# Stage A of a spectral mixing kernel: casts ahead of copies, other engines for the copies, fewer warming matmuls, one placement moved

## The chip, the cores and the metric

The kernel runs on one core of a Trainium2 chip. The time is the device time of that core in microseconds (us). Before the change it was 764.62 us, the median of three runs (763.43, 764.62, 766.18). The profiled execution has a span of 763.7 us from its first to its last instruction. Engines are called by their names: TensorE (PE in the profile, PEld for its weight loads), VectorE (DVE), ScalarE (ACT), GpSimd (POOL), and SyncE (SP), which issues transfers.

## The reference

Two layers follow each other. The first mixes along the sequence with a filter in the frequency domain, the second is a feed-forward layer with a squared ReLU. In short:

```
X = np.fft.rfft(x, axis=1)                         # x: 8 x 3008 x 256, float32
Y = X * (filt_r + 1j * filt_i)[None]               # filt_r, filt_i: 1505 x 256
y = np.fft.irfft(Y, n=3008, axis=1)
h = np.maximum(y.reshape(24064, 256) @ w_in, 0.0)  # w_in: 256 x 2048
out = h * h @ w_out                                # w_out: 2048 x 256
```

## The kernel before

**The whole.** The sequence length is 3008 = 64 x 47, so the transform is done in two stages with matrices of sines and cosines: stage A transforms along 47, stage B along 64, then comes the product with the filter (`prods`, line 423), and two inverse stages (`unit_p0` or `unit_p`, line 446 or 460, and `unit_y`, line 496). The result `yt` goes into the feed-forward part, 47 groups of 512 tokens. All tiles between are float16. For seven of the eight batches the transform is woven into the feed-forward steps by a plan (`fft_plan`) that gives each unit a due step. Batch 0 has nothing to hide behind: its transform, and the setup of all constants, is the prologue, which takes the first 58 us of the profiled execution and is written out by hand at the end of the kernel. The change lies in this prologue alone.

**Queues.** [...] The order of the calls in lines 738 to 808 is therefore also the order of each engine's queue[...].

**Stage A of batch 0.** x of batch 0 is loaded as float32 into three tiles `xw` (0, 1, 2), each in two halves of 512 KB, in the order of `HALVES`: (0,0), (1,0), (0,1), (1,1), (2,0), (2,1). SyncE issues these six transfers first, then the filter's real and imaginary parts (1504 KB each), small constants, the constants of stage B (`sSB`, `sSP`), and `w_in`. `cast_wide` (line 226) turns a half into float16 on VectorE. Eight units, `unit_a0(c, k)` with c from 0 to 3 and k of 0 or 1, do the transform: each has 16 matmuls of 96 columns (lines 373 and 375) into two banks of PSUM. Units with c of 0 or 2 read `xw16` of tile 0, those with c of 1 or 3 tile 2; all read tile 1 too. The two banks are copied into the tile `uT`: where they are one `psH` tile, both by ScalarE (line 382) or both by VectorE (line 384), in turn; where they are a pair of `psF` or `psO`, the first by ScalarE and the second by VectorE.

**After stage A.** `turn_u(k, eng)`, six times, transposes `uT` by matmuls with the identity (line 392, `psT`) and copies it into `ut` (lines 398 and 400). The filter is cast to float16 in pieces (line 222): the real part by GpSimd and VectorE, the imaginary part by VectorE, GpSimd and ScalarE. `place_f(im, k, ...)` puts a sixth of the real (im 0) or imaginary part (im 1) where stage B's output wants it: matmuls with a selection matrix (line 286, `psf`), then an evacuation into `sF` by ScalarE (line 294) or VectorE (line 298). A placement of the imaginary part needs all three pieces of that part's cast.

**The rounds.** The loop over k from 0 to 6 at line 785 holds two `unit_b` (two matmuls, line 415, and one product on VectorE, line 423), the next imaginary placement, from the second round on a `unit_p0` with its evacuation `ze` on ScalarE (line 448), and in the first three rounds a real placement. `unit_p0` also reads `sSPx`, constants with swapped halves that GpSimd copies (lines 778 and 779), between loads of batch 1. After the rounds `read_z`, four `unit_a` of batch 1, 13 filling matmuls and four `unit_y` lead into the feed-forward loop (line 526).

**Banks of PSUM.** `bank_pair` (line 169) deals out pairs of banks in rotation: two tiles of `psH` (each one tile of two banks, so one evacuation), then a pair of `psF`, then a pair of `psO` (two tiles, so two evacuations). Every `unit_a0`, every `turn_u` and the placements ahead of the rounds take the next pair. Counting from 0, the eight units take 0 to 7, the six turns 8 to 13, the placements ahead of the rounds 14 to 17. Placements inside the rounds and `unit_p0` take `psH`; `unit_b` of batch 0 takes `psF` or `psO`.

**Warming.** While x is on its way, TensorE runs `WARM` matmuls of 512 columns on zeros (line 265).

The functions and the calls follow, with the line numbers of the profile.

Of the kernel before, what the change touches and what calls it, by code (L numbers as in the profile page):

```python
# [20 lines left out]
SLOTS = 8  # L21
CLS = 376
QF = 3008
WARM = 16


def _build_consts():
# [83 lines left out]
def kernel(  # L111
# [9 lines left out]
    nc = tc.nc  # L121
# [38 lines left out]
    def psO(name):  # L160
        return pps.tile([128, 2, 256], F32, tag="psO", name=name, bufs=2)

    def psH(name):
        return pps.tile([128, 2, 512], F32, tag="psH", name=name, bufs=2)
# [4 lines left out]
    def bank_pair(name):  # L169

        k = npair[0] % 4
        npair[0] += 1
        if k < 2:
            t = psH(name)
            return [t[:, 0, :], t[:, 1, :]], [(t, 0)]
        ts = [psF(f"{name}_{i}") if k == 2 else psO(f"{name}_{i}").rearrange("p a d -> p (a d)")
              for i in range(2)]
        return ts, [(t.unsqueeze(1), i) for i, t in enumerate(ts)]

    def pair_engine():  # L180
        return nc.vector if npair[0] % 2 == 0 else nc.scalar
# [39 lines left out]
    def cast(eng, out, in_):  # L221
        (eng.copy if eng is nc.scalar else eng.tensor_copy)(out=out, in_=in_)

    def cast_wide(k, i):
        m = slice(4 * i, 4 * i + 4)
        nc.vector.tensor_copy(out=xw16[k][:, m, :], in_=xw32[k][:, m, :])

    HALVES = ((0, 0), (1, 0), (0, 1), (1, 1), (2, 0), (2, 1))
# [34 lines left out]
    ps = psO("warm").rearrange("p a d -> p (a d)")  # L263
    for _ in range(WARM):
        nc.tensor.matmul(ps, zero, sF[:, 0, 0:2, :], start=True, stop=True)  # L265
# [3 lines left out]
    def place_f(im, k, *engs, rotate=False):  # L269

        if rotate:
            banks, groups = bank_pair(f"psf_{im}_{k}")
        else:
            t = psH(f"psf_{im}_{k}")
            banks, groups = [t[:, 0, :], t[:, 1, :]], [(t, 0)]
        for i in range(4):
            c = 4 * k + i
            e0, e1 = D * c, D * (47 - c)
            cuts = [0] + [d for d in range(1, D)
                          if (e0 + d) % QF == 0 or (c and (e1 + d) % QF == 0)] + [D]  # L280
            for d0, d1 in zip(cuts, cuts[1:]):
                o = banks[i // 2][:, (i % 2) * D + d0:(i % 2) * D + d1]
                low = divmod(e0 + d0, QF)
                up = divmod(e1 + d0, QF) if c else (0, QF + d0)
                for r, (q, a) in enumerate((low, up, low, up)):
                    nc.tensor.matmul(o[32 * r:32 * r + 32, :], sPF[:, q, :],  # L286
                                     f16s[0][:, im, a:a + d1 - d0], start=True, stop=True)
        for t, i in groups:
            n = t.shape[1]
            eng = engs[i % len(engs)]  # L290
            dst = sF[:, im, 4 * k + 2 * i:4 * k + 2 * i + 2 * n, :]
            src = t.rearrange("p t (a d) -> p (t a) d", d=D)
            if eng is nc.scalar:
                eng.activation(out=dst, in_=src, func=AF.Copy, scale=sign[:, 0:1] if im else 1.0)
            elif im:
                eng.tensor_scalar_mul(out=dst, in0=src, scalar1=sign[:, 0:1])
            else:
                eng.tensor_copy(out=dst, in_=src)
# [4 lines left out]
    def load_win():  # L303

        for k, c, n, pool, tag in ((0, 0, 768, p_ze, "ze"), (0, 768, 768, p_ze, "ze"),
                                   (0, 1536, 512, p_prod, "prod"), (1, 0, 768, p_ze, "ze"),
                                   (1, 768, 512, p_prod, "prod"), (1, 1280, 512, p_prod, "prod"),
                                   (1, 1792, 256, p_prod, "prod")):
            t = pool.tile([128, n], F32, tag=tag, name=f"win32_{k}_{c}")
            nc.sync.dma_start(out=t, in_=moe_w_in[128 * k:128 * k + 128, c:c + n])  # L310
            wins.append((t, k, slice(c, c + n)))
# [50 lines left out]
        if b == 1:  # L362
            write_u(b, c)

    def unit_a0(c, k):

        banks, groups = bank_pair(f"psA_0_{c}_{k}")
        for dt in range(2):
            for i in range(4):
                m = 4 * k + i  # L370
                o = banks[dt][:, 96 * i:96 * i + 96]
                d = slice(128 * dt, 128 * dt + 128)
                nc.tensor.matmul(o, xw16[2 * (c % 2)][:, m, d], s0[:, c // 2, :],  # L373
                                 start=True, stop=False)
                nc.tensor.matmul(o, xw16[1][0:120, m, d], s0[0:120, 2 + c, :],
                                 start=False, stop=True)
        for dt in range(2):
            m = 32 * c + 16 * k
            o = uT[:, dt, :, m:m + 16].rearrange("p c (m q) -> p m c q", q=4)
            pv = banks[dt][:, 0:384].rearrange("p (m c q) -> p m c q", m=4, q=4)  # L380
            if (pair_engine() is nc.scalar) if len(groups) == 1 else (dt == 0):
                nc.scalar.copy(out=o, in_=pv)
            else:
                nc.vector.tensor_copy(out=o, in_=pv)

    def turn_u(k, eng):

# [21 lines left out]
    def unit_b(b, p):  # L409
        if b == 0 and p % 4 > 1:  # L410
            ps = psO(f"psB_{b}_{p}").rearrange("p a d -> p (a d)")
        else:
            ps = psF(f"psB_{b}_{p}")
        for i in range(2):
            nc.tensor.matmul(ps[:, i * D:(i + 1) * D], sSB[:, 2 * p + i, :],  # L415
                             uts[b][:, 2 * p + i, :], start=True, stop=True)
        if b == 0:
            if p == 0:
                prods["ring"] = p_y.tile([128, 5, 2, 2, D], F16, tag="yt", name="prods_0")
            prod = prods["ring"][:, p % 5]  # L420
        else:
            prod = p_prod.tile([128, 2, 2, D], F16, tag="prod", name=f"prod_{b}_{p}")
        nc.vector.tensor_mul(  # L423
            out=prod,
            in0=ps.rearrange("p (a d) -> p a d", d=D).unsqueeze(1).to_broadcast([128, 2, 2, D]),
            in1=sF[:, :, 2 * p:2 * p + 2, :])
        prods[(b, p)] = prod
        if b > 0:
            for i in range(2):
                nc.gpsimd.dma_start(out=prod[64 * i:64 * i + 64, 0],  # L430
                                    in_=prod[64 - 64 * i:128 - 64 * i, 1],
                                    accum_op=mybir.AluOpType.add)
# [3 lines left out]
    def unit_p0(k):  # L436

        if k == 0:
            zes[0] = p_h2.tile([128, NC, D], F16, tag="h2", name="ze_0")
        ze = zes[0][:, 4 * k:4 * k + 4, :]  # L440
        ps = psH(f"psP_0_{k}")
        for i in range(4):
            c2 = 4 * k + i
            prod = prods[(0, c2 // 2)]
            for v, w in enumerate((sSP[:, c2, :], sSPx[c2 // 12][:, c2 % 12, :])):
                nc.tensor.matmul(ps[:, i // 2, (i % 2) * D:(i % 2) * D + D], w,  # L446
                                 prod[:, v, i % 2, :], start=(v == 0), stop=(v == 1))
        nc.scalar.copy(out=ze, in_=ps.rearrange("p t (a d) -> p (t a) d", d=D))
        nc.sync.dma_start(
            out=dZ[0].rearrange("(s p) d -> p s d", p=128)[:, 4 * k:4 * k + 4, :],  # L450
            in_=ze)
# [286 lines left out]
    for k in range(2):  # L738
        c = slice(12 * k, 12 * k + 12)
        load_const(sSB[:, c, :], dSB, k)  # L740
        load_const(sSP[:, c, :], dSP, k)
    load_win()
    for k, i in HALVES[:2]:
        cast_wide(k, i)
    unit_a0(0, 0)
    unit_a0(2, 0)
    for k, i in HALVES[2:4]:
        cast_wide(k, i)
    unit_a0(0, 1)
    unit_a0(2, 1)  # L750
    for i in range(2):
        cast_wide(2, i)
        unit_a0(1, i)
        unit_a0(3, i)
    f16s.append(p_h2.tile([128, 2, QF + D], F16, tag="h2", name="f16"))
    for im in range(2):
        nc.gpsimd.tensor_copy(out=f16s[0][:, im, QF:], in_=nyq[:, im, :])
# [8 lines left out]
    turn_u(5, nc.vector)  # L766
    place_f(0, 0, nc.scalar, rotate=True)
    place_f(0, 1, nc.vector, rotate=True)
    place_f(0, 2, nc.scalar, rotate=True)
    for eng, e in ((nc.vector, slice(0, 1024)), (nc.gpsimd, slice(1024, 2048)),  # L770
                   (nc.scalar, slice(2048, QF))):
        cast(eng, f16s[0][:, 1, e], f32s[1][:, e])
# [1 line left out]
    for k in range(6):  # L774
        if k % 3 == 0:
            sSPx.append(p_u.tile([128, 12, 128], F16, tag="u", name=f"sSPx_{k}"))
        c, o = slice(4 * k, 4 * k + 4), slice(4 * k % 12, 4 * k % 12 + 4)
# [7 lines left out]
    for k in range(7):  # L785
        if k < 6:
            unit_b(0, 2 * k)
            if k < 5:
                place_f(1, k + 1, nc.scalar)
            unit_b(0, 2 * k + 1)  # L790
        if k > 0:
            unit_p0(k - 1)
        if k < 3:
            place_f(0, k + 3, nc.scalar)
    read_z(0, 0)
    read_z(0, 1)
    tiny = const.tile([1, 1], F16, name="tiny")
# [16 lines left out]
    for s in range((NG + 1) * SLOTS):  # L814
        g, k = divmod(s, SLOTS)
# [16 lines left out]
        while stores and stores[0][0] <= s:  # L832
            _, i, n, ost = stores.pop(0)
# [31 lines left out]
```

## Time and profile before

| What | Value |
|---|---|
| median time of three runs | 764.62 us |
| span of the profiled execution | 763.7 us |
| TensorE busy, whole span | 742.6 us (97%) |
| TensorE busy, first 60 us | 46.61 us |
| VectorE busy, first 60 us | 36.56 us |
| ScalarE busy, first 60 us | 31.97 us |
| GpSimd busy, first 60 us | 23.40 us |
| mean granted TensorE clock, first 60 us | 0.89 |
| first matmul of stage A | 9.02 us |
| first turn (psT) | 22.89 us |
| first product of batch 0 (prods) | 33.77 us |
| last ze evacuation of batch 0 starts | 49.56 us |
| first feed-forward matmul (psH) | 58.17 us |

The busy shares of a page are means over the whole span, and the prologue is under a tenth of it. It is therefore read from the timeline of each engine: every line has a start, a length, the engine, the source line, output and inputs, the number of merged instructions, and in brackets the idle time ahead of it with what ended it. The view of waits sums such idle times by the pair of who waited and for what. The chain of work that ended last goes back from the last instruction, at each step to what released it; in order of time its lines have a start, a length and what ran. SPq is the queue of SyncE, in which an issue can wait for a transfer that was issued earlier.

### The profile page before, as it was taken

How to read it: one execution, taken by the hardware profiler on the slowest of the kernel's cores; microseconds unless marked ns; L12 is line 12 of the kernel's file. 1: busy time of each engine (PE TensorE's matmuls, PEld its weight loads, DVE VectorE, ACT ScalarE, POOL GpSimd, SP SyncE). 2: the span in 40 equal slices, each digit the busy share in tenths (PEclk: the TensorE clock that was granted, in tenths of full speed). 3: DMA queues.
4: the chain of work that ended last, by engine and by line, in shares of the span. 5: the costliest groups of instructions: out<-in, count | busy, mean ns of one | idle time of the engine just before them, and what ended most of it. 6: DMA issues, size and time to landing. Idle time of an engine off the chain costs nothing.

```text
span 763.7 us, 20209 instructions
## 1 busy us (share of the span) xinstructions
PE 742.6 (97%) x8517; PEld 539.8 (71%) x8517; DVE 656.9 (86%) x732; ACT 563.9 (74%) x803; POOL 191.4 (25%) x265
## 2 busy tenths in 40 slices
PE   6789899999999999999999999999999999999998
PEld 4555666767777776877778777787767777777776
DVE  4677997899989998998989999899989989888773
ACT  2677678777877777787777877777777777777673
POOL 0920561043303232223212324043311222000000
PEclk9799999999999999999999999999999999999999
DMA  9968599657676556854577555865447334321011
GB/s 351 267 160 226 86 188 218 185 108 153 133 220 126 102 112 157 219 124 96 126 179 176 116 124 106 216 140 111 101 116 204 88 73 98 97 74 53 30 56 57
DMA packets 103459, 106.36 MB, mean 139 GB/s; under 512 B 10320, under 2 KB 93520, under 8 KB 102216
## 3 DMA queue, kind: packets, MB, share of 16 engines
q1 hardware_dynamic: 83928, 81.83, 35.4%
q0 software_dynamic: 19296, 23.05, 21.8%
q8 instruction: 67, 1.10, 0.6%
q10 hardware_dynamic: 144, 0.18, 0.1%
q14 instruction: 24, 0.20, 0.1%
HBM read 57.80 MB, written 48.23 MB: 139 GB/s over the span
## 4 chain that ended last, share of the span: by engine, by line
PE 90%; DVE 5%; DMA 2%; ACT 1%; issue 1%; SPq 0%; ACTq 0%; DVEq 0%
PE psH L526 40%; PE psX L641 21%; PE psY L641 16%; PE psB L415 3%; PE psY L496 3%; PE psP L460 2%; PE psA L347 2%; DVE prod L423 1%; PE psO L546 1%; PE warm L265 1%; DVE h L537 1%; DMA dU<-u 1%; PE psf L286 1%; PE psP L446 1%; PE psA L373 1%
## 5 line engine op out<-in xcount | busy, mean ns | idle before, releaser
L530 ACT ACTIVATE h<-psH 128x1024 f16<-128x1024 f32 x376 | 384.9, 1025 | 160.4 <-PE psH L526 158.9
L526 PE MATMUL psH<-yt,sWin 128*128 128x512 f16 (+7 forms) x1728 | 386.8, 351 | 1.2 <-ACT h L530 0.4
L537 DVE TENSOR_TENSOR h<-h 128x2048 f16<-128x2048 f16 (+1 forms) x192 | 229.7, 1197 | 45.7 <-ACT h L530 45.5
L430 POOL DMA_DIRECT2D prod<-prod x168 | 138.7, 968 | 428.3 <-DVE prod L423 425.9
L526 PEld LDWEIGHTS <-sWin 128*128 128x128 f16 x1728 | 149.1, 98 | 90.5 <-issue 3.0
L641 PEld LDWEIGHTS <-sum 128*128 128x128 f16 x2944 | 181.3, 98 | 26.1 <-issue 6.3
L641 PEld LDWEIGHTS <-h 128*128 128x128 f16 x2208 | 135.6, 98 | 24.5 <-issue 5.3
L423 DVE TENSOR_TENSOR prod<-psB,sF 128x1024 f16<-128x1024 f32 x84 | 102.2, 1218 | 11.9 <-PE psB L415 11.8
L641 PE MATMUL psX<-sT,sum 128*128 128x128 f16 x1472 | 104.7, 219 | 0.0
L641 PE MATMUL psY<-sT,sum 128*128 128x128 f16 x736 | 71.2, 219 | 0.0
L641 PE MATMUL psY<-sWout,sum 128*128 128x128 f16 x736 | 56.0, 219 | 1.4 <-DVE bot L656 1.4
L615 DVE TENSOR_TENSOR sum<-sum,h 128x2048 f16<-128x2048 f16 x46 | 56.1, 1220 | 0.8
L195 POOL DMA_DIRECT2D x<-in_x_dram x64 | 56.3, 1053 | 0.5 <-PE psA L347 0.5
L641 PE MATMUL psY<-sWout,h 128*128 128x128 f16 x736 | 56.2, 219 | 0.0
L641 PE MATMUL psX<-sT,h 128*128 128x128 f16 x736 | 56.1, 219 | 0.0
L618 DVE TENSOR_TENSOR sum<-h 128x2048 f16<-128x2048 f16 x46 | 55.9, 1216 | 0.0
L621 DVE TENSOR_TENSOR sum<-h,sum 128x2048 f16<-128x2048 f16 x46 | 55.9, 1215 | 0.0
L612 DVE TENSOR_TENSOR sum<-h 128x2048 f16<-128x2048 f16 x46 | 55.9, 1215 | 0.0
L462 ACT CAST ze<-psP 128x512 f16<-128x512 f32 x84 | 49.2, 586 | 1.2 <-PE psP L460 1.0
L641 PE MATMUL psX<-sWout,h 128*128 128x128 f16 x736 | 48.7, 219 | 0.0
L505 DVE CAST yt<-psY 128x376 f16<-128x376 f32 x62 | 33.6, 542 | 14.0 <-PE psY L496 13.8
L496 PE MATMUL psY<-sC,zt 112*128 112x94 f16 x512 | 42.3, 204 | 0.9 <-DMA zt<-dZ 0.5
(75 smaller groups left out, 558.1 us busy)
## 6 DMA issues: line engine op xcount, KB each, us to landing
zt<-dZ SPq DMA_DIRECT2D x64, 192.0 KB
dU<-u SPq DMA_DIRECT2D x56, 192.0 KB
prod<-prod POOLq DMA_DIRECT2D x168, 64.0 KB, 2.9
dZ<-ze SPq DMA_DIRECT2D x28, 384.0 KB
x<-in_x_dram POOLq DMA_DIRECT2D x48, 192.0 KB, 5.1
ut<-dU SPq DMA_DIRECT2D x7, 1024.0 KB
out_dram<-bot SPq DMA_DIRECT2D x32, 128.0 KB
out_dram<-top SPq DMA_DIRECT2D x16, 256.0 KB
```

What stands on the lines that cost most here:

```text
L195: nc.gpsimd.dma_start(out=t[64 * h + p0:64 * h + p1], in_=v[p0:p1, 8 * c:8 * c + 8, :])
L423: nc.vector.tensor_mul(out=prod, in0=ps.rearrange("p (a d) -> p a d", d=D).unsqueeze(1).to_broadcast([128, 2, 2, D]), in1=sF[:, :, 2 * p:2 ...
L430: nc.gpsimd.dma_start(out=prod[64 * i:64 * i + 64, 0], in_=prod[64 - 64 * i:128 - 64 * i, 1], accum_op=mybir.AluOpType.add)
L496: nc.tensor.matmul(ps[:, 94 * jj:94 * jj + 94], zt[:, 4 * (g % 2) + jj, dt * 128:(dt + 1) * 128], sSY, start=True, stop=True)
L526: nc.tensor.matmul(ps[:, i, o:o + n], sWin[:, dt, jt * 128:(jt + 1) * 128], yts[b][:, dt, r:r + n], start=(dt == 0), stop=(dt == 1))
L530: nc.scalar.activation(out=h2[:, 2 * s:2 * s + 2, :], in_=ps, func=AF.Relu)
L537: nc.vector.tensor_mul(out=v, in0=v, in1=v)
L612: nc.vector.tensor_add(out=t, in0=a21, in1=a22)
L615: nc.vector.tensor_sub(out=t, in0=f[5], in1=a11)
L618: nc.vector.tensor_sub(out=t, in0=a11, in1=a21)
L621: nc.vector.tensor_sub(out=t, in0=a12, in1=f[6])
L641: nc.tensor.matmul(o[:, t, :], f[p][:, q, 128 * t:128 * t + 128], sg["w"][p][:, q, :], start=(m == 0 and p in (1, 2)), stop=(q == 7), skip ...
```

## The change

Four edits, all ahead of the rounds:

1. All six casts of x stand ahead of any copy in VectorE's queue, so that each can run when its half has arrived.
2. `unit_a0` is told which engine copies each bank. The first four units (c of 0 and 2) are copied by ScalarE alone; the last four by VectorE (first bank) and ScalarE (second bank). The matmuls' order stays.
3. Ten warming matmuls instead of sixteen, so that TensorE is free earlier.
4. The fourth real placement, `place_f(0, 3)`, moves from the first round to ahead of the rounds; the real placements in the rounds come in rounds 0 and 1 instead of 0 to 2. As it takes bank pair 17, the first imaginary placement takes pair 18, which is a pair of `psF`, and its evacuation falls into two, one on ScalarE and one on VectorE.

```diff
-WARM = 16
+WARM = 10
...
-    def unit_a0(c, k):
+    def unit_a0(c, k, *engs):
...
-            if (pair_engine() is nc.scalar) if len(groups) == 1 else (dt == 0):
-                nc.scalar.copy(out=o, in_=pv)
-            else:
-                nc.vector.tensor_copy(out=o, in_=pv)
+            cast(engs[dt], o, pv)
...
-    for k, i in HALVES[:2]:
+    for k, i in HALVES:
         cast_wide(k, i)
-    unit_a0(0, 0)
-    unit_a0(2, 0)
-    for k, i in HALVES[2:4]:
-        cast_wide(k, i)
-    unit_a0(0, 1)
-    unit_a0(2, 1)
-    for i in range(2):
-        cast_wide(2, i)
-        unit_a0(1, i)
-        unit_a0(3, i)
+    for c, i in ((0, 0), (2, 0), (0, 1), (2, 1)):
+        unit_a0(c, i, nc.scalar, nc.scalar)
+    for c, i in ((1, 0), (3, 0), (1, 1), (3, 1)):
+        unit_a0(c, i, nc.vector, nc.scalar)
...
     place_f(0, 1, nc.vector, rotate=True)
-    place_f(0, 2, nc.scalar, rotate=True)
+    for k in (2, 3):
+        place_f(0, k, nc.scalar, rotate=True)
...
-        if k < 3:
-            place_f(0, k + 3, nc.scalar)
+        if k < 2:
+            place_f(0, k + 4, nc.scalar)
```

## The prediction

> **What bounds the kernel now.** I read the busy shares first, then the chain that ended last, then the order of time on VectorE, SyncE's queue and TensorE inside the first 36 us, where all edits lie.
>
> ```profile
> PE 742.6 (97%) x8517; PEld 539.8 (71%) x8517; DVE 656.9 (86%) x732; ACT 563.9 (74%) x803; POOL 191.4 (25%) x265
> PE 90%; DVE 5%; DMA 2%; ACT 1%; issue 1%; SPq 0%; ACTq 0%; DVEq 0%
> ```
>
> From about 58 us on, TensorE is the chain almost without a break, and nothing there is edited. So the question is how much earlier the feed-forward part can begin: a time saved ahead of it is passed on whole unless something ahead of it doesn't move along. The chain in order of time shows what sets the pace ahead of it (start, length, what):
>
> ```profile
> 10.66 1.02 DVE uT L384 x2
> 11.68 1.21 DVE xw L226 x2
> 12.94 0.22 PE psA L375
> ...
> 14.54 0.56 DVE uT L384
> 15.10 0.61 DVE xw L226
> 15.76 0.26 PE psA L373
> ...
> 18.54 1.02 DVE uT L384 x2
> 19.56 0.61 DVE xw L226
> ...
> 31.24 0.61 DVE f L222
> 31.90 0.62 PE psf L286 x16
> ```
>
> It is a ladder: VectorE copies one group's results, only then casts the next half of x, TensorE computes on it, VectorE copies. Did the halves arrive that late? SyncE's queue tells: its issues of line 736 each wait for one more half of x (four waits, in the view of waits), so their starts date the landings.
>
> ```profile
> 8.34 0.33 SPq L736 DMA_DIRECT2D sSB<-cSB  x1
> 9.46 0.32 SPq L736 DMA_DIRECT2D sSP<-cSP  x1
> 10.72 0.32 SPq L736 DMA_DIRECT2D sSB<-cSB  x1
> 12.00 0.32 SPq L736 DMA_DIRECT2D sSP<-cSP  x1
> ```
>
> The third to sixth half are there at 8.3, 9.4, 10.7 and 12.0 us. Their casts start at 11.6, about 12.2, 15.02 and 19.48: the last waits 7.5 us behind copies in VectorE's queue. The same reading of line 310's waits gives the filter: real part at 15.6, imaginary part at 19.4 us. In one-microsecond stretches the granted clock is 1.00 up to 15, 0.50 from 16 to 25, and 1.00 again at 26; line 373 follows line 375 at 45 ns in the first and at 80 ns in the second.
>
> [...] 0.50 follows 12 to 15.3, in which TensorE worked some 1.8 us, and ends after 22 to 25.5, in which it worked nearly all the time. The warming matmuls start 0.43 us apart, and the last weight loads come closer together from about 8.6 us, some 6 us after the first: there the clock rose. [...] the trace: 1024 columns from SBUF in 0.69 us, 384 from PSUM in 0.56.
>
> **The change, part by part.**
>
> *Casts ahead.* Six casts of 0.69, each now at its landing (a landing was followed by its cast within 0.1 us for the first two): they end at 5.8, 7.2, 9.0, 10.15, 11.4 and 12.7. Nothing is added; VectorE was idle for 3.44 us ahead of its first copy.
>
> *Warming.* Ten instead of sixteen at 0.43: the end moves from about 9.0 to 6.95, so the first unit can start at 7.26, when the second half is cast. The clock is then still half. [...]
>
> *Stage A.* A unit is 16 matmuls: 0.72 us at 45 ns, 1.28 at 80. Units (0,0) and (2,0): 7.26 to 8.5 and 9.3. Then a wait for the fourth half's cast: units (0,1), (2,1) 10.2 to 11.7. Then (1,0), (3,0) after 11.45: 11.7 to 13.15. Then (1,1), (3,1): 13.15 to 14.6. ScalarE has now 12 copies, in pairs of 0.86 (0.43 each), 0.48 alone: first unit 8.75 to 9.65, second to 10.5, third 11.2 to 12.05, fourth to 12.9, then four single ones, the last at 14.85 to 15.3. That is 5.4 us of copies in 6.6 us, with slack. VectorE's four, 0.47 to 0.56 each, follow its last cast and end with unit (3,1)'s, at 14.8 + 0.56 = 15.35. [...] **Turns start at 15.35** instead of 23.6 (the second psT; the first came at 22.89).
>
> *Turns to the filter casts.* At full clock two turns are 16 matmuls by 56 ns, so VectorE's first turn copy starts 1.1 us later, at 16.5, where it took 25.43 - 23.61 = 1.8 at half clock. From there VectorE ran without a gap from 25.43 to 31.84 (1.14 + 1.07 + 2.33 + 1.20 + 0.67 by the starts): that is 6.4, so 22.9. Its filter cast at 17.6 finds the real part (15.6); GpSimd's half, released by the last cast of x at 12.7 instead of 20.2, is done by 15.6 + 1.44 = 17.1. The imaginary part is there at 19.4, so GpSimd's third is done at 20.5. The filter hides behind VectorE, by 2 to 3 us: no new bound.
>
> *The placement moved ahead.* It costs 0.62 us of TensorE, between others, and one ScalarE evacuation of 1.02. ScalarE's order is: third placement, fourth placement, its piece of the imaginary cast. Before, that piece ended at 31.76, with VectorE's (31.84), so ScalarE had no slack and the new evacuation goes on the path: third placement 20.95 to 21.95, fourth (its bank is free when VectorE's last turn copy ends at 21.1, matmuls to 21.75 or 22.1) to 23.1, cast to **24.1**, against 22.9 without it: 1.2.
>
> *Side effect: banks.* Pairs rotate by four, so the extra placement shifts the first imaginary one from the two-bank tile to the psF pair. Its evacuation splits: ScalarE 0.6, VectorE 0.67 (row of L298) in parallel, instead of 1.11 on ScalarE. But unit_b's first product uses psF too, so its matmuls (0.54), which ran during the evacuation, now follow it. Together 0.1 worse, and the second imaginary placement, queued behind those matmuls on TensorE, comes some 0.7 later against the first product. First product: 24.15 + 0.65 to 0.95 (matmuls) + 0.7 + 0.55 = 26.1 to 26.5, so **26.3** instead of 33.77: 7.5 earlier.
>
> *Rounds.* VectorE's 12 products need 12 x 1.215 = 14.6 us; they took 15.1 (33.77 to 48.89), with 0.38 and 0.68 of gaps where ScalarE's evacuations held a psH bank. One 1.02 fewer in the rounds, less the 0.7 above, leaves the gaps about as they are: 15.0 to 15.2. I book nothing. GpSimd's swapped constants, which end block by block from 24.66 to 35.92, don't move along with the rest, since its transfers and the constants' landings keep their times; but the block for round i is needed only at 29.3, 32.4, 35.4, 37.6, 38.9, 41.4 (lines 446 shifted by 7.5), so each is there. Its weight casts end at 41.2 and are needed at about 50.7.
>
> *Sum:* 7.5 earlier, less 0.1 for small things: 764.6 - 7.4 = **757.2**.
>
> **Rivals.**
>
> *The clock stays half in stage A*[...]. Units take 1.28: 7.26 to 9.8, 10.2 to 12.8, on to 17.9, the turns at 18.7 and VectorE's first turn copy 1.8 later at 20.5: 4.9 ahead of 25.43, less 1.3 for the placement and the banks: 3.6, so 761.0. [...]
>
> *The gain is lost on the way*, in stage B's writes and reads through DRAM, or the feed-forward part starts early and then waits for batch 1's transfers (the chain has 5.69 and 3.84 us of them at 62 to 72). Then nothing or little is left: 764. Against: these transfers are issued behind the evacuations and move with them, and the transfer engines are nearly idle at 36 to 38, so no backlog reaches them.
>
> *Slower: ScalarE's longer list serialises stage A*, each unit waiting for the copies of the one before: 8 x (1.28 + 0.9) = 17.4 from 7.3, so turns at 24.7, 1.1 later than now, plus 1.3 for placement and banks: 767. Against: four pairs of banks rotate, so a unit waits for the copies of the fourth before it.
>
> *Better:* the placement hides after all, and the rounds close their gaps: 1.2 + 0.9 more, 755.1.
>
> **Chances.** Forecast (756 to 758.5) 0.60, half clock in part or whole (758.5 to 761) 0.20, better 0.11, lost 0.05, slower 0.04. For 8 in 10 I take the forecast's case and most of those beside it: 755.2 to 760.3. Faster by over 0.3% (2.3 us) is the first three and a sliver of the fourth: 0.92; within 0.3%: 0.04; slower 0.04.
>
> **What would show it.** Casts of L226 end by 12.8; psA's last matmul at about 14.6 and the first psT near 15.4; clock 1.00 from 8.6 to about 19; four sF evacuations of the real part by ScalarE and VectorE ahead of its imaginary cast, and this cast the last of three; first prods at 26.3; last ze, at 49.56 before, at about 42; first psH, at 58.17, at about 51. If psT starts at 17 to 19 with matmuls of stage A 80 ns apart, the warming was too short. If psT is early but prods aren't, I mis-read the middle part. If psH is early and the end isn't, the loss lies in the feed-forward part, and the prediction is wrong there.

## The result and the profile after

The changed kernel takes **759.95 us** (median of four runs, 759.59 to 761.15). The kernel before, measured beside it, has 764.59 us. The ratio is 0.9941, with a 95% interval of 0.9919 to 0.9962: faster by 4.6 us or 0.6%. The prediction was 757.2 in a range of 755.2 to 760.3. So the direction and the range were right, and 2.8 us of the expected 7.4 did not arrive. Where they went is the subject of what follows.

The profiled executions differ by 6.1 us (spans of 763.7 and 757.6). That of before lies 0.9 above its median and that of after 0.4 below its own, so the two traces show some 1.3 us more than the medians.

The busy shares of the changed kernel's page are within one per cent of those before, and so are the shares of the chain; transfers and ScalarE have one more per cent each:

```profile
PE 89%; DVE 5%; DMA 3%; ACT 2%; issue 1%; POOL 0%; SPq 0%; DVEq 0%; ACTq 0%
```

The ladder is gone. This is VectorE's timeline in the changed kernel (start, length, engine, line, operation, tiles, count, and the idle time ahead with what ended it):

```profile
8.27 0.69 DVE L226 CAST xw<-xw 128x1024 f16<-128x1024 f32 x1 [1.05 <-DMA xw<-in_x_dram]
9.50 0.69 DVE L226 CAST xw<-xw 128x1024 f16<-128x1024 f32 x1 [0.54 <-DMA xw<-in_x_dram]
...
12.04 0.69 DVE L226 CAST xw<-xw 128x1024 f16<-128x1024 f32 x1 [0.58 <-DMA xw<-in_x_dram]
12.65 2.28 DVE L222 CAST uT<-psA 128x384 f16<-128x384 f32 x4
...
25.05 13.81 DVE L420 TENSOR_TENSOR prods<-psB,sF 128x1024 f16<-128x1024 f32 x12 [0.35 <-PE psB L412]
```

Each cast now waits for its half of x and for nothing else, and the twelve products run without a gap. The first turn's matmul starts at 14.98 us instead of 22.89, the first product at 25.05 instead of 33.77. The last evacuation of the rounds (`ze`, which is then written to DRAM as `dZ` and read back as `zt`) starts at 39.54 instead of 49.56. **At the end of the rounds the change is 10.0 us ahead**, more than forecast. Then the lead melts. These are pieces of the chain in order of time, first of the kernel before, then of the changed one (start, length, what):

```profile
49.56 1.02 ACT ze L448
...
50.60 2.42 DMA dZ<-ze
...
53.16 3.43 DMA zt<-dZ
...
56.72 0.33 PE psY L496 x4
```

```profile
39.54 1.02 ACT ze L445
40.58 5.50 DMA dZ<-ze
46.23 3.13 DMA zt<-dZ
...
49.49 0.33 PE psY L493 x4
```

The write of the last `ze` into DRAM takes 5.50 us instead of 2.42; the read behind it takes no longer than before. The first psY with data (the matmuls of `unit_y`, which read `zt`) is 7.2 us ahead, no longer 10.0. In the view of waits, TensorE's wait for this read has grown from

```profile
PE psY L496 <- DMA zt<-dZ: 0.5, 1, 0.5
```

to

```profile
PE psY L493 <- DMA zt<-dZ: 3.3, 1, 3.3
```

A second, smaller loss comes behind it. TensorE has nothing to do in those 3.3 us, and soon after the granted clock is halved for some 3 us. The stretches of the changed kernel, with busy time and instructions of each engine, then the clock, the transfer engines' share and GB/s:

```profile
46.30:49.50 3.20, 0.01 (x1) 0.04 (x2) 0.00 (x0) 0.00 (x0) 1.07 (x2) 1.00 0.78 149
49.50:54.00 4.50, 4.30 (x30) 2.17 (x31) 1.10 (x2) 1.97 (x3) 0.00 (x0) 0.62 1.13 189
```

The first h (ScalarE's evacuation of psH) starts at 52.85 instead of 59.37, 6.5 ahead. The half clock is not over by then. TensorE's timeline shows the first 20 matmuls of psH, in the changed kernel and in a later kernel (e1 below) in which TensorE hardly waits and the clock stays at 1.00:

```profile
50.94 4.18 PE L523 MATMUL psH<-yt,sWin 128*128 128x512 f16 x12 [0.20 <-ACT yt L500]
55.37 1.94 PE L523 MATMUL psH<-yt,sWin 128*128 128x512 f16 x8 [0.25 <-ACT h L527]
```

```profile
48.96 2.04 PE L523 MATMUL psH<-yt,sWin 128*128 128x512 f16 x8 [0.28 <-ACT yt L500]
51.24 1.94 PE L523 MATMUL psH<-yt,sWin 128*128 128x512 f16 x8 [0.25 <-ACT h L527]
53.38 1.02 PE L523 MATMUL psH<-yt,sWin 128*128 128x512 f16 x4 [0.20 <-ACT h L527]
```

From the first psY to the 21st matmul of psH it is 8.0 us in the changed kernel, and 6.9 both before and in e1. So this stretch takes 1.1 us of the lead and leaves 6.1, which is also the lead of the last h (745.8 instead of 751.9).

### The profile page after: what moved, and what is told of

The parts are those of the page before. It is cut to its first block, busy times and chain, and to the rows that moved or that the text cites. A ratio compares the mean times of both kernels' runs of the same rounds, so it can differ in the third digit from the quotient of the medians.

```text
span 757.6 us, 20196 instructions
## 1 busy us (share of the span) xinstructions
PE 737.0 (97%) x8511; PEld 536.0 (71%) x8511; DVE 655.4 (87%) x729; ACT 564.6 (75%) x807; POOL 191.0 (25%) x265
## 4 chain that ended last, share of the span: by engine, by line
PE 89%; DVE 5%; DMA 3%; ACT 2%; issue 1%; POOL 0%; SPq 0%; DVEq 0%; ACTq 0%
PE psH L523 40%; PE psX L638 21%; PE psY L638 16%; PE psB L412 3%; PE psY L493 3%; PE psP L457 2%; PE psA L347 2%; DVE prod L420 1%; DMA xw<-in_x_dram 1%; PE psO L543 1%; DVE h L534 1%; ACT h L527 1%; DMA dZ<-ze 1%; PE psf L286 1%; PE psP L443 1%
## 5 line engine op out<-in xcount | busy, mean ns | idle before, releaser
L534 DVE TENSOR_TENSOR h<-h 128x2048 f16<-128x2048 f16 (+1 forms) x192 | 229.7, 1197 | 46.6 <-ACT h L527 46.1
```

The costliest lines, as they stand in the source:

```text
L534: nc.vector.tensor_mul(out=v, in0=v, in1=v)
```

## The experiments

Each kernel was timed beside the kernel before on the same chip, and the ratios are to that. A profile shows one execution, and it can lie off the kernel's median: 1.8 us above it in e5, 1.9 in e4, 3.2 in e2. Traces of the same code also differ: up to the first product e8 is the kernel before, and this product came at 32.77 us in its trace and at 33.77 in the other. So a difference of about 1 us between two traces says little unless it repeats.

The theory at the start: the lead is lost on the transfer engines, because the load of the first half of `w_out` (`load_wout(0)`, issued by GpSimd in the rounds) kept its time while the rounds moved up to it. The rival: the six writes of the rounds, packed closer together, hold up each other.

### The weight load moved behind the rounds (e1)

```diff
-    load_wout(0)
     cast_win()
...
+    load_wout(0)
     load_wout(1)
```

> The changed kernel with the first weight load (sWout, first half) issued next to the second, after batch 0's first read_z, instead of during the rounds. Theory A (the 10 us won by the end of the rounds shrink to 7 because that load stands on the transfer engines together with the last dZ writes): the last dZ write lands in 2.5 to 3.5 us instead of 5.5, the first real psY starts near 47.5 instead of 49.5, and the time is 1.5 to 2.5 us under the changed kernel's 759.95, so about 758. Theory B (the six dZ writes, packed into 11 us, hold up each other): the last dZ write still takes 5 us, psY stays at 49.5, the time at 760.

Measured: 757.04 us, ratio 0.9901 (0.9886 to 0.9917). The chain in order of time of this kernel:

```profile
40.66 1.02 ACT ze L445
...
41.70 2.38 DMA dZ<-ze
...
44.22 3.15 DMA zt<-dZ
...
47.51 0.33 PE psY L493 x4
```

The last write is back at 2.38 us, although the six writes are as close together as before, and psY starts at 47.5. This kernel even ended its rounds 1.1 us later than the changed one, and still had psY 2.0 earlier. What stood in the way can be seen in the transfers between 38 and 42 us. The columns are packets, MB, and the share of the 16 engines' time. Queue q0 is GpSimd's, q1 SyncE's. First the changed kernel, then e1:

```profile
q0 software_dynamic: 885, 0.45, 93.7%
q1 hardware_dynamic: 694, 0.35, 31.1%
```

```profile
q1 hardware_dynamic: 1263, 0.63, 51.6%
...
q0 software_dynamic: 1, 0.00, 0.0%
```

In the changed kernel the weight load occupies the engines in the stretch in which the last writes of the rounds want them, and it landed at 44.8 us. In e1 it is gone from there. The rival falls. Over the last write's own 5.5 us (40.6 to 46.1), though, the packets of the load's queue took only 20.7% of the engines' time and those of SyncE's queue 59.7%. That points to a backlog: SyncE moved 0.35 MB from 38 to 42 us, against 0.63 in e1, and in those 5.5 us it moved 0.98 MB, of which the last write is 0.26. How the delay divides between the load itself and this backlog is not shown; that it goes when the load goes is.

The moved load returns the second loss as well. In e1 TensorE waits 0.2 us for the read instead of 3.3, the clock stays at 1.00, and the 2.0 us at psY have become 3.1 at the 21st matmul of psH.

### The control: the same move in the kernel before (e8)

> The kernel before with nothing but the moved weight load: the control. Theory A (in the kernel before the load had landed long ahead of the last dZ write, which took 2.4 us): nothing to gain, 764.5 within 0.7, first psY at 56.7. Theory B (the moved load helps the feed-forward part or any prologue): 762 or less, and then the moved load says nothing on where this change's 2.8 us went.

Measured: 764.96 us, ratio 1.0001 (0.9990 to 1.0011). Moving the load gains nothing by itself: the last write took 2.43 us with it and 2.42 without it. Before the change, the load had the same stretch, 38 to 42 us, nearly to itself:

```profile
q0 software_dynamic: 1005, 0.51, 100.5%
q1 hardware_dynamic: 480, 0.24, 20.4%
```

The last write came at 50.6 then, long after it. The first psY of e8 is 1.2 us earlier than before, but 1.0 of that is there at the first product, ahead of the load. So the load's place became a cost only through this change. This cost is shown: e1 is 2.9 us under the changed kernel by the medians and 3.1 by the ratios, and the two intervals do not meet. It is as large as the missing 2.8 us, although it is not the only difference from the forecast (see below).

### The casts alone (e5) and with the moved load (e7)

```diff
-    for k, i in HALVES[:2]:
+    for k, i in HALVES:
         cast_wide(k, i)
     unit_a0(0, 0)
...
-    for k, i in HALVES[2:4]:
-        cast_wide(k, i)
...
-        cast_wide(2, i)
         unit_a0(1, i)
```

> The kernel before with one edit: all six casts of x ahead of the copies (engines of the copies, 16 warming matmuls and placements as before). Theory A (the order in VectorE's queue is the whole ladder): units follow the landings, psT near 16 instead of 22.9, first product near 26.5, and the end of the rounds at about 43; less 1.5 to 3 lost behind the rounds: 760.5. Theory B (the copies by VectorE behind the last cast at 12.7 are a ladder of their own, so the new engines are needed): the copies of the first four units, which wait for the casts, hold their banks, psT comes at 18 or later, and the time is 762 or above.

Measured: 759.71 us, ratio 0.9943 (0.9929 to 0.9957), the same as the whole change. psT started at 16.15, the first product at 25.97, the last `ze` at 41.76. VectorE's copies do pile up behind the last cast, but they don't delay much, as its timeline shows:

```profile
12.80 3.80 DVE L384 CAST uT<-psA 128x384 f16<-128x384 f32 x8
17.70 1.22 DVE L400 CAST ut<-psT 128x1024 f16<-128x1024 f32 x1 [1.10 <-PE psT L392]
```

Eight copies take 3.80 us against four in 2.28 with the new engines: 1.5 us, of which 1.2 is seen at psT. Theory A holds. In its profile this kernel ends its rounds 2.2 us later than the changed kernel, and its last write took less (4.57 us), so that psY comes only 1.3 later. That profile also took 1.9 us longer than the changed kernel's, while the medians are equal, so it does not show why they are. But the load could hide what the other three edits are worth, and e7 takes it away:

> The kernel before with the casts ahead alone (as in the earlier run of that edit) and the first weight load moved behind the rounds. Theory A (the other three edits do bring the rounds to their end some 2 us earlier, and only the transfers behind hid it): the rounds end at 41.8 to 43, first psY at 48.7 to 50, time 758.5 to 759.3, which is 1.5 to 2.3 us above the full change with the moved load (757.0). Theory B (the other three edits are worth nothing): 757.0, the same as with all four.

Measured: 757.97 us, ratio 0.9908 (0.9895 to 0.9922), against 0.9901 (0.9886 to 0.9917) with all four edits. Neither theory is met. The medians differ by 0.9 us, the intervals overlap, and the first psY differs by 1.25 (48.76 and 47.51). By the medians the other three edits bring about 1 us; the intervals leave room for nothing and for some 2 us. What repeats in the traces is the end of stage A: psT starts between 14.86 and 15.02 in all eight profiles with the new engines of the copies, with ten or sixteen warming matmuls, and at 16.15 and 16.01 with the casts alone. So the new engines bring some 1.1 us there, and whether it reaches the end is not shown.

### Fewer warming matmuls (e6, e4, e10)

In the kernel before, `WARM = 10` alone (e6):

> The kernel before with one edit: 10 warming matmuls instead of 16. Theory A (VectorE's queue order sets the pace): the first copies end 1.7 us earlier, each cast behind them too as far as its half is there; psT at 21.2 to 22.5, time 763 to 764.5. Theory B (the clock doesn't rise with ten): stage A's first matmuls 80 ns apart, psT not earlier, time 764.6 or above.

Measured: 764.92 us, ratio 1.0009 (1.0001 to 1.0017). Stage A started at 6.92 instead of 9.02, but psT at 22.24 instead of 22.89, and in e8, with sixteen, at 22.02. So an earlier start of TensorE did not show at psT, as theory A had it; the time lies in theory B's range and is, if anything, 0.1% above the kernel before. The clock also fell to half earlier: in e6 stage A's matmuls were 80 ns apart by 11.3 us, where before the clock was halved at 15.4 (by 14.0 in e8); 80 ns instead of 45 is their distance at half clock, as the prediction read. This run therefore doesn't separate a pace set by VectorE from one set by the clock. That the order in VectorE's queue is at the root is shown by e5, in which nothing else was changed and the last cast of x started at 12.19 instead of 19.48: there the clock stays at 1.00 through stage A too. In the changed kernel, `WARM = 16` (e4):

> The changed kernel with 16 warming matmuls as before. Theory A (fewer warming matmuls matter little, since the last half of x lands at 12.0 anyway and ScalarE has slack): stage A starts at 9.0, its first four units end at 11.9, the last psA at 14.7 to 15.2, psT 0.3 to 0.6 later than now, the time within 0.5 us of 760. Theory B (each of the eight ScalarE copies is on the path): stage A's end comes 1.7 us later, and the time is 761.5.

Measured: 760.07 us, ratio 0.9943 (0.9929 to 0.9958). Stage A started at 7.73 and not at 9.0, psT at 14.93 and the first product at 25.00, so theory A holds, with less delay than stated. With the moved load (e10):

> The changed kernel with the moved weight load and 16 warming matmuls. Theory A (stage A waits for the halves of x, not for TensorE to be free): psT at 14.9, time 757 within 0.5. Theory B (a longer warming makes up for something that the transfers hid): time differs from 757.0 by over 0.7.

Measured: 757.74 us, ratio 0.9905 (0.9883 to 0.9926), against 0.9901 with ten. psT started at 15.00. The medians differ by 0.7, at the edge between the two theories and within wide intervals. The six runs go from 755.71 to 760.53 us, and their granted clocks go with them, from 1.000 in the fastest to 0.993 in the slowest; nothing in the profile ties that to the warming. No difference between ten and sixteen is shown.

### The placement moved back (e3, e9)

```diff
-    for k in (2, 3):
-        place_f(0, k, nc.scalar, rotate=True)
+    place_f(0, 2, nc.scalar, rotate=True)
...
-        if k < 2:
-            place_f(0, k + 4, nc.scalar)
+        if k < 3:
+            place_f(0, k + 3, nc.scalar)
```

> The changed kernel with the fourth real placement back in the first round. Theory A, the account of the prediction (the placement ahead costs 1.2 us of ScalarE before the first product, and the rounds gain nothing by it): first product at 23.8 instead of 25.05, rounds 15.1 long, end of the rounds 38.9 as now or earlier. Theory B (the placement ahead pays, because it takes ScalarE off the rounds' path: 13.8 instead of 15.1 us for 12 products): first product 24.0, last one ends at 39.1 or later, so moving it changed nothing in sum. In both the time is 760 within 0.5, as the transfers behind the rounds absorb such differences.

Measured: 761.81 us, ratio 0.9959 (0.9944 to 0.9974). The first product came at 24.48, 0.57 earlier than with the placement ahead. The twelve products then took 14.1 us, and the last `ze` started at 39.26, 0.3 earlier. The end of the rounds is thus about the same, as theory B had it, with a smaller cost ahead than theory A said. (This edit also gives the first imaginary placement its one `psH` tile back, so 0.57 holds that side effect too.) The median is 1.9 above the changed kernel, which neither theory expected. In this profile the last write took 5.98 us, and the clock was halved from 48 to 55 us instead of 50 to 53, so that the way from the first psY to the 21st matmul of psH took 8.9 us instead of 8.0. By the ratios the difference is 1.4 us, and the intervals overlap, so I don't take it for an effect of the placement, and with the moved load it is not there:

> The changed kernel with the moved weight load and the fourth real placement back in the first round. Theory A (the moved placement shifts ScalarE's work from the rounds to ahead of them and no more): first product 0.6 earlier and rounds longer by as much, time 757 within 0.5. Theory B (it pays, because a placement in the rounds holds a psH bank there): time 758 or above.

Measured: 756.95 us, ratio 0.9889 (0.9875 to 0.9904), against 0.9901 and 757.04 with the placement ahead. The first product came at 24.47 instead of 24.92 and the last `ze` at 40.28 instead of 40.66, so the rounds are not longer by as much. The time is theory A's: the moved placement shifts work and gains nothing that these runs show.

### More filling matmuls ahead of unit_y (e2)

```diff
-    for _ in range(13):
+    for _ in range(28):
```

> The changed kernel with 28 instead of 13 filling matmuls ahead of unit_y, so that TensorE works while it waits for zt (3.3 us idle). Theory A (this idle time is what halves the clock at 50.7 to 53.6 and so delays the first feed-forward steps): the clock stays 1.00, the first h ends at about 53.2 instead of 53.9, the time is 0.7 us lower, 759.2. Theory B (the first steps wait for something else later, so the clock costs nothing): 760.

Measured: 760.15 us, ratio 0.9943 (0.9926 to 0.9961). The time doesn't separate the theories. The clock stayed at 1.00 once psY had begun, but in the profile the fillings themselves became the bound. TensorE's timeline of this execution, the slowest of the six (763.36 us):

```profile
45.90 7.00 PE L796 MATMUL fill<-sSB,zero 128*128 128x512 f16 x28
...
52.85 0.33 PE L493 MATMUL psY<-sC,zt 112*128 112x94 f16 x4
```

Here twenty-eight were too many: they took 7.00 us, part of it at half clock (0.50 from 45 to 47 us), and psY no longer waited for the read. The traces answer what the time doesn't. From the first psY to the 21st matmul of psH it is 6.9 us here too. This way is 6.89 to 6.91 us in the eight profiles (before, e1, e2, e6 to e10) in which TensorE waited at most 0.5 us for the read and the clock was not halved behind it. It is 8.0 to 9.2 in the four in which TensorE waited 2.3 to 4.5 us (the changed kernel, e3, e4, e5); in each of these the clock was halved there. So the halved clock costs 1.1 us or more on this way, and theory B, by which it costs nothing, doesn't hold.

### Matmuls on zeros between the placements (e11)

In the profiles of e1, e2, e5, e7, e9 and e10 the clock was 0.50 somewhere between 23 and 31 us. In those of the changed kernel, e3 and e4 it was not. The last kernel is e1 with seven matmuls on zeros after the fourth real placement:

```diff
+    ps = psO("keep").rearrange("p a d -> p (a d)")
+    for _ in range(7):
+        nc.tensor.matmul(ps, zero, sSB[:, 0:4, :].rearrange("p a b -> p (a b)"),
+                         start=True, stop=True)
```

> The changed kernel with the moved weight load, and seven matmuls on zeros (512 columns, 0.22 us each, 1.5 in all) after the fourth real placement, where TensorE otherwise waits for the casts of the filter's imaginary part. In several profiles with early rounds the clock was 0.50 between some 24 and 28 us, and the 12 products then took 14.4 to 15.1 us instead of 13.8. Theory A (this is the few matmuls from 20 to 24 us): the clock stays 1.00 through the rounds, products take 13.8, first psY at 46.3 instead of 47.5, time 756.0. Theory B (the fillings delay the imaginary placement by 0.3 or more, and the clock falls elsewhere): 757 or above.

Measured: 756.03 us, ratio 0.9878 (0.9861 to 0.9894), the lowest of all. The same stretches in e1 and in e11 (first PE busy, then PEld, DVE, ACT, POOL; the clock is the third number from the end):

```profile
20.00:24.00 4.00, 1.87 (x55) 1.00 (x45) 2.56 (x5) 3.22 (x4) 2.43 (x4) 1.00 1.04 415
24.00:28.00 4.00, 3.67 (x46) 1.56 (x49) 3.18 (x4) 2.15 (x3) 3.83 (x8) 0.59 1.07 380
```

```profile
20.00:24.00 4.00, 3.43 (x66) 1.89 (x62) 3.58 (x6) 3.33 (x5) 2.13 (x2) 1.00 1.03 414
24.00:28.00 4.00, 3.38 (x67) 1.83 (x70) 2.63 (x3) 2.58 (x4) 3.83 (x9) 1.00 1.07 380
```

The clock stays at 1.00 for the whole prologue, and the products take 13.81 us instead of the 15.1 from 24.92 to 39.98 in e1. That much of theory A holds. It repeats beyond the profile: the granted clock over the whole execution is 1.000 in all four runs of e11, and 0.997 or 0.998 in the four of e1. In the profiled execution the real part of the filter came later (GpSimd's cast of it started at 17.23 instead of 15.62, ahead of the added matmuls), so that the first product came at 26.12, and psY was not earlier than in e1. The median is 1.0 lower and the intervals overlap, so that the gain over e1 is likely and not shown.

## Why the prediction was right, and where it was not

**Casts ahead and stage A: right.** The casts end within 0.1 us of the stated times. The last psA matmul starts at 14.49 (14.6 forecast), psT at 14.98 (15.35), and the granted clock is 1.00 from stage A to the end of the rounds. That the clock would be up by then, and would stay up, was an estimate. The measured rise came earlier than the forecast's 8.6: the warming matmuls started 0.43 us apart up to 6.06, and what followed came 0.23 behind. The first matmul of stage A started at 6.5, so the warming ended before the forecast's 6.95, and the matmuls were 45 ns apart from 7.3 on. The rival of a clock at half rate through stage A did not occur in any profile with the casts ahead; with sixteen warming matmuls nothing changes. The longest gap of TensorE in stage A was 1.0 us, and the clock stayed at 1.00 behind it; in e1 it was halved later on, at 24.7 us, behind gaps of at most 1.2, and behind a gap of 1.17 in the changed kernel (up to 22.56 us) it was not. So the length of a gap alone does not tell whether the clock stays up. The casts alone bring as much as the change (e5), and what the other edits add is not resolved.

**Turns to the first product: 1.25 too late.** 26.3 was forecast, 25.05 measured. Of this, 0.4 was there at psT. The fourth placement was put at 1.2 us of path and its side effect at 0.1; together they cost 0.57 (e3). VectorE's filter cast took 0.93 instead of 1.16 (0.93 in e8 too, so not through the change), and the imaginary placement ran at full clock (the sixteen matmuls of the second took 0.62 us instead of 1.04). That ScalarE's piece of the cast would be the last of the three, through the placement ahead, is what the chain shows:

```profile
22.47 0.89 ACT f L222
23.40 0.31 PE psf L286 x3
```

**Rounds: 1.3 too long.** "I book nothing" was wrong for the profiled execution. The products closed up to 13.8 us, and most of that is the clock: where it was halved in these same rounds they took 15.1 (e1, e10). With the placement back they took 14.1 at full clock (e3) and 15.1 with a halved one (e9). So the clock is worth 1.0 to 1.3 us there, and the placement 0.3. The prediction put the gaps of before down to ScalarE's evacuations. It did not look at the clock in these rounds, which was halved there too, as a stretch of the kernel before shows (the clock, 0.50, is the third number from the end):

```profile
34.00:35.00 1.00, 1.00 (x22) 0.53 (x22) 1.00 (x2) 0.92 (x1) 0.94 (x2) 0.50 0.72 139
```

Its floor of 12 x 1.215 = 14.6 was too high as well. A product takes 1.2 us, but the next one starts 1.15 us after it; twelve without a gap are the 13.81 of the changed kernel.

**The failed step: the way behind the rounds.** The forecast gave the rival of a gain lost on the way 0.05, with the words "the transfer engines are nearly idle at 36 to 38, so no backlog reaches them". That looked at the wrong stretch. The weight load ran from 38 to 42 us in the kernel before, where nothing on the path waited for it; and it is issued by GpSimd after its constants and loads, which, as the prediction itself said, "don't move along with the rest". It was issued 1.2 us earlier while the last write moved 10.0 us earlier, into it. The prediction asked whether GpSimd's results are there in time, and not what its transfers would meet. The runs show the price: 3.1 us on the last write, of which the moved load returns all (e1), and nothing of it exists without the change (e8). Another 1.1 us went to the clock that was halved behind this wait, which the forecast did not have.

**The sum.** By the profiles: 8.7 at the first product, 1.3 in the rounds, less 2.8 for the write and the read, less 1.1 at half clock, makes 6.1. Less the 1.3 by which the two executions lie off their medians it is 4.8, against 4.6 measured. That the time lies in the stated range is partly luck. The end of the rounds came 2.5 us earlier than forecast, and 3.9 us were lost behind it that the forecast did not have. And the part of the range in which 759.95 lies, 758.5 and above, had been given to the half clock in stage A, which did not occur. With the load out of the way, the change gives 757.04, near the 757.2 of the forecast; but the forecast reached that with a smaller lead and no loss, and e1 lost some of its rounds to the clock.

**Open.** What the three other edits are worth together, about 1 us by the medians, is below what these runs resolve. How the delay of the last write divides between the load and the backlog behind it was not tested, and neither was why the clock is halved in the rounds of one execution and not of another.

## What to carry to other kernels

When a stage moves up, list what does not move with it: transfers and casts whose time is set by another engine's queue. Then look at the stretch into which the end of the stage is moved, not at the one from which it came. A transfer that costs nothing in a profile can cost microseconds (3.1 here) once something else is in a hurry beside it, and as it has slack it can be put elsewhere. And of several edits made together, the one that frees a queue's order may be nearly all of the gain; each of the others needs a run of its own before it is kept for its reason.

## What the runs showed of the hardware

- The load of half of `w_out`, 512 KB written as float16, held the 16 transfer engines for some 4 us (0.51 MB at 100.5% of their time, 38 to 42 us in the kernel before). A write of 256 KB beside it took 5.5 us instead of 2.4, and the load itself landed 10.2 us after its issue instead of 5.8.
- The clock does not need a long pause of TensorE to be halved. With TensorE busy for 1.87 of 4 us (20 to 24 in e1) and no pause above 1.2 us it was halved at 24.7. With 2.02 of 4 in e10 it was halved too; with 2.00 in the changed kernel, 1.95 in e4 and 1.91 in e3 it was not, so the busy share of these 4 us doesn't decide it. With 3.43 of 4 (e11) it stayed up. The changed kernel and e2 have the same code until behind the rounds, and only in the profile of e2 was the clock halved, from 23.6 us on. So the same code gets a halved clock in one execution and not in another. Why, the runs do not show. In the six profiles in which it was halved between 23 and 26 us (e1, e2, e5, e7, e9, e10), TensorE was busy for 1.51 to 2.02 us of the 4 from 20 to 24.
- A wait of TensorE behind the rounds was followed by a halved clock in all four profiles in which it was 2.3 to 4.5 us long, and in none of the nine in which it was at most 0.6 (there the granted clock was 1.00 behind it, or, in e6 and e8, the first eight matmuls of psH took 2.03 us, as they did at 1.00 in the kernel before). From the first psY to the 21st matmul of psH it took 8.0 to 9.2 us in those four instead of 6.9.
